# Attention two batches at a time, single heads on 64 partitions, 32-blocks solved by outer products, the order set by a list scheduler

## The chip, the core and the metric

The kernel runs on one core of a Trainium2 chip. A core has TensorE (PE, with weight loads shown as PEld), VectorE (DVE), ScalarE (ACT), GpSimd (POOL) and SyncE (SP), which here does nothing but issue DMAs. The metric is the time of one execution in microseconds (us) on the device. Time before: median 1033.7 us over three runs (1032.56 to 1038.22).

## The reference

A recurrence over 768 tokens, for 4 batches and 8 heads of 40 channels, and then a product over all 3072 tokens of 320 channels:

```python
for t in range(S):                                   # S = 768, state is 40x40 per batch and head
    y[:, :, t] = np.einsum('bhd,bhde->bhe', rt, state)
    Sa = np.einsum('bhde,bhe->bhd', state, at)
    state_decay = state * wt[:, :, None, :] - np.einsum('bhd,bhe->bhde', Sa, bt)
    state = state_decay + np.einsum('bhd,bhe->bhde', vt, kt)
x = y.transpose(0, 2, 1, 3).reshape(3072, 320)
out = ((x @ w_a) * (x @ w_b)) @ w_out                # d_ff = 1536; the weights are float64
```

## The kernel before

The recurrence runs in 12 chunks of 64 tokens. For a chunk, *prep* forms the running products of the decays (scans `Pc`, `Qc` on DVE), multiplies them into a, b and k (`A`, `BK`), transposes b and k (`bkn`) and makes the scores of b and k against a. The scores of a head are a 64x64 triangular matrix; `I + it` has to be inverted. *lanes* inverts its two 32x32 diagonal blocks, *merge* makes the block beside them from two products, and *main* computes, in turn: `RH` (state and v met by a), `UV` (the inverse times that), `G` (masked products of r), `yn` (the output), the new state `ST`, and its transpose `SD`. *xform* and *expand* turn y into x, split in a high and a low float32r part (`xk`, 120 rows of three heads).

Before, each of the four batches is prepared and run by itself. Three heads share 120 partitions, and a product that must keep heads apart uses an operand that is laid out block-diagonally (`Abd`, the state `ST`, the decays `pcm`; POOL makes them). `lanes` has the 128 blocks of a chunk on lanes: 64 blocks, each on two lanes which take every second row. Its 31 steps are a multiplication (L504) and a subtraction (L507) on DVE. Its data goes out through DRAM and back (`nb_d` to `N`, `Y` to `ts_d` to `TT`).

The product after it runs in *units*: one tile of 128 of the d_ff channels for the 256 tokens of a chunk. A unit is 16 matmuls into `ab`, copies and one product on ACT and DVE (`asb`, `g`, `gh`), a subtraction on POOL (`gl`) and 6 matmuls into `po`. There are 12 tiles and 12 chunks: 144 units. The first four tiles (`F1 = 4`) run beside the attention; the sums are put into DRAM (`po_d`), as is x (`xk_d`). In the last stage x and sums are loaded again, and the other eight tiles run in groups of two, over all chunks. The float64 weights are decoded on the chip to a high and a low part, in 72 pieces of 192 or 160 columns (six operations on DVE, two on ACT, two on POOL); `fill_rows` copies some rows within SBUF (`wt<-wt`).

The order is written out by times: a table `DEF` gives each step of prep, lanes, merge, main and units an emission time within a chunk of 16 units of time, the steps are sorted by it (`events`), and the engines' instructions are emitted in that order. Lane steps wait in a list (`fill`) and go behind other DVE instructions one at a time. All DMAs are issued by SP, in program order; each waits for its inputs and for room at its target, and holds back what stands behind it.

Of the kernel before, what the change touches and what calls it, by code (L numbers as in the profile page):

```python
# [30 lines left out]
CW = NG * (C + 1)      # width of the decay part of a packed input tile  # L31
PW = CW + 1 + NG * 3 * C
F1 = 4         # d_ff tiles that run beside the attention
FG = 2         # d_ff tiles of a group afterwards

LIMIT = 2.0 ** 8       # sum of the squares of the factors, over 2^60, that the chunked form may meet

# emission times of the parts of a step, 16 to a step, 4 to a batch
DEF = {
# [8 lines left out]
}  # L48


class InOrder:
    """An engine whose instructions keep the order in which they are given; after() comes
    behind each."""

    def __init__(self, tc, eng):
        self.tc, self.eng, self.after = tc, eng, None

    def __getattr__(self, name):
        fn = getattr(self.eng, name)

        def call(*args, **kwargs):
            r = fn(*args, **kwargs)  # L62
            self.tc.keep_in_program_order(r)
            if self.after:
                self.after()
            return r
        return call


def token_by_token(tc, p, ps_at, pin, rv, done):  # L70
    """The recurrence as it stands, a token at a time; done(n, x) gets x^T of a chunk."""
    nc = tc.nc
    # 1 where row and column belong to the same head
# [8 lines left out]
    # identity for the rows of each head  # L82
# [30 lines left out]
    with tc.For_i(0, pin.shape[0], 1) as n:  # L113
        I = p.tile([PK, B, PW], F32, name="sI")
        nc.sync.dma_start(out=I, in_=pin[bass.ds(n, 1)].rearrange("n b p w -> p (n b) w"))
        # in the order of the packed input: v, r and, in the order of the other groups, b and k of the second
        V, R, BK = (p.tile([PK, B, x, C], F32, name=nm) for nm, x in (("sV", NG), ("sR", NG), ("sBK", 2)))
        for g in range(NG):
            for t, x in ((V, 4 if g == 1 else 0), (R, 3 if g == 1 else 4)):
                nc.sync.dma_start(  # L120
                    out=t[:, :, g], in_=rv[bass.ds(n, 1), :, :, (1, 0, 2)[g], x].rearrange("n b p t -> p (n b) t"))
        abk = I[:, :, CW + 1:].rearrange("p b (g x t) -> p b g x t", g=NG, x=3)
        for i in range(2):
            nc.vector.tensor_copy(out=BK[:, :, i], in_=abk[:, :, 1, 2 - i])
        nc.vector.tensor_copy(out=abk[:, :, 1, 1:], in_=BK)
        x = p.tile([PK, NG, B, C], F32, name="sx")
        w = I[:, :, 0:CW].rearrange("p b (g t) -> p b g t", t=C + 1)
        for t in range(C):
            a, b, k = (abk[:, :, :, i, t] for i in range(3))
            rs, vs = columns(R[:, :, :, t], "r"), columns(V[:, :, :, t], "v")  # L130
# [8 lines left out]
            nc.vector.tensor_mul(out=state, in0=state, in1=rows(w[:, :, :, t + 1]))  # L139
# [10 lines left out]
def wkv_moe(ctx, tc, pin, rv, vn, wa, wb, wo, out):  # L150
# [4 lines left out]
    WIDE = wo.dtype == I64  # L155

    const = ctx.enter_context(tc.tile_pool(name="const", bufs=1))
    dram = ctx.enter_context(tc.tile_pool(name="dram", bufs=1, space=DRAM))
    psab = ctx.enter_context(tc.tile_pool(name="psab", bufs=2, space=PSUM))
    pso = ctx.enter_context(tc.tile_pool(name="pso", bufs=2, space=PSUM))  # L160
    psa = ctx.enter_context(tc.tile_pool(name="psa", bufs=4, space=PSUM))

    def ps_at(name):
        return psa.tile([P, 512], F32, tag="at", name=name)
# [23 lines left out]
    # 1 where the row belongs to head j of its group  # L188
    m3 = const.tile([PK, NG], F32, name="m3")
    nc.gpsimd.memset(m3, 1.0)  # L190
    nc.gpsimd.affine_select(
        out=m3, in_=m3, pattern=[[-D, NG]], compare_op=ALU.is_ge, fill=0.0,
        base=0, channel_multiplier=1)
    nc.gpsimd.affine_select(
        out=m3, in_=m3, pattern=[[D, NG]], compare_op=ALU.is_gt, fill=0.0,
        base=D, channel_multiplier=-1)
# [4 lines left out]
    yid = const.tile([P, HB // 2, HB], F32, name="yid")  # L201
    nc.gpsimd.memset(yid, 1.0)
    for p in range(2):
        sl = yid[p * 64:(p + 1) * 64]
        nc.gpsimd.affine_select(
            out=sl, in_=sl, pattern=[[2, HB // 2], [-1, HB]], compare_op=ALU.is_equal,
            fill=0.0, base=p, channel_multiplier=0)
    sizes = const.tile([PK, 2 * B * NS], F32, name="sizes")
    usual = const.tile([1, 1], I32, name="usual")
    ones = const.tile([PK, 1], F32, name="ones")  # L210
    nc.gpsimd.memset(ones, 1.0)
    # DRAM scratch
    xk_d = [dram.tile([PK, 6, B * C], F32, name=f"xk_d{n}") for n in range(NS)]
    po_d = [dram.tile([2, P, DM], F32, name=f"po_d{n}") for n in range(NS)]
    nb0_d = [dram.tile([B * H, HB, HB], F32, name=f"nb0_d{n}") for n in range(NS)]
    nb1_d = [dram.tile([B * H, HB, HB], F32, name=f"nb1_d{n}") for n in range(NS)]
    ts_d = [dram.tile([2, B * H, HB, HB], F32, name=f"ts_d{n}") for n in range(NS)]

    def decode(pool, raw, rows, ncol, dst_hi, dst_lo):
        """High and low parts of float64 words, or of float32 values."""  # L220
        def t(name, dt=I32):
            return pool.tile([P, 192], dt, tag=name, name=name, bufs=2)[:rows, 0:ncol]

        def shaped(x):
            return x.rearrange("p (k f) -> p k f", k=3) if len(dst_hi.shape) == 3 else x

        if not WIDE:
            yield
            nc.scalar.copy(out=dst_hi, in_=shaped(raw))
            nc.vector.tensor_sub(out=dst_lo, in0=shaped(raw), in1=dst_hi.bitcast(F32))  # L230
            yield
        low, high = raw[:, :, 0], raw[:, :, 1]
        ex, mt, rs = t("w_ex"), t("w_mt"), t("w_rs")
# [3 lines left out]
        ts(out=ex, in0=high, scalar1=0x7FF00000, scalar2=None, op0=ALU.bitwise_and)  # L237
        nc.scalar.activation(out=ex, in_=ex, func=AF.Relu, scale=8.0, bias=bias[:rows])
        ts(out=mt, in0=high, scalar1=3, scalar2=0x007FFFF8, op0=ALU.logical_shift_left, op1=ALU.bitwise_and)
# [37 lines left out]
    def weights(dest):  # L277
# [4 lines left out]
        for i, (f, j, h) in enumerate(pieces):  # L282
            yield
            if begun:
                next(begun)
# [707 lines left out]
```

## Time and profile before

| | before |
|---|---|
| median of three runs | 1033.7 us |
| profiled execution, span | 1042.0 us, mean granted TensorE clock 0.899 |
| PE, PEld | 915.3 us (88%), 832.5 us (80%) |
| DVE | 692.4 us (66%) |
| ACT, POOL | 411.0 us (39%), 426.1 us (41%) |
| DMA | 103.29 MB in 135747 packets, 84922 of them under 512 B |

Busy times are those of one execution taken by the profiler; the time of a run is what the device takes without it. A row such as `L507 DVE TENSOR_TENSOR Y<-Y,Yt 128x126 ... x372 | 138.3, 372 | 8.5` is one group of instructions: line, engine, operation, output from inputs, partitions by elements of one form, count, busy us, mean ns of one, and idle time of its engine just ahead of it. In a row for a queue (`SPq`) three numbers are the shortest, the median and the longest duration of an issue in ns, which is the time that SP takes to hand over the DMA and not the time of its transfer. In a table by stretches each row has a stretch from:to in us, its length, the busy time of each engine with its count, the TensorE clock that was granted, the mean busy share of the 16 DMA engines, and GB/s.

### The profile page before, as it was taken

The page shows a single profiled execution, that of the slowest core. Times are in us where ns is not written, and L with a number is a line of the kernel's source. Part 1 is how long each engine was busy: PE and PEld are TensorE (multiplying, and loading weights), DVE is VectorE, ACT ScalarE, POOL GpSimd, SP SyncE. Part 2 cuts the span into 40 slices and gives each one's busy share as a digit, 9 for nine tenths or more (in the row PEclk, how much of TensorE's full clock was granted, in tenths as well). Part 3 has the DMA queues.
Part 4 walks back from the last instruction along what each step waited for, and adds up shares of the span by engine and source line. Part 5 has one row for each costly group of instructions (what it writes and reads, how often), then busy time and mean ns, then how long its engine had stood idle before and what let it go on. Part 6 is the DMA issues. An engine that isn't in the chain of part 4 may idle for free.

```text
span 1042.0 us, 23609 instructions
## 1 busy us (share of the span) xinstructions
PE 915.3 (88%) x8942; PEld 832.5 (80%) x8942; DVE 692.4 (66%) x1890; ACT 411.0 (39%) x1317; POOL 426.1 (41%) x655
## 2 busy tenths in 40 slices
PE   4347798799999999999999999998939999999997
PEld 3236687688888888888888888877939999999996
DVE  7849889887869694859695937256227676757322
ACT  2122454444444444444544433345314343334221
POOL 5423647444435443434443402034215454445321
PEclk9999757889999988898989879797969999999998
DMA  3344544727364636363636242343873110110111
GB/s 72 73 103 111 119 123 106 171 58 167 99 151 113 146 100 140 82 139 115 134 104 140 84 96 85 73 133 97 202 185 88 32 43 24 39 31 25 39 57 62
DMA packets 135747, 103.29 MB, mean 99 GB/s; under 512 B 84922, under 2 KB 125690, under 8 KB 135626
## 3 DMA queue, kind: packets, MB, share of 16 engines
q1 hardware_dynamic: 135626, 101.71, 39.6%
q8 instruction: 73, 1.20, 0.5%
q14 instruction: 48, 0.39, 0.1%
HBM read 77.77 MB, written 21.94 MB: 96 GB/s over the span
## 4 chain that ended last, share of the span: by engine, by line
PE 46%; DVE 31%; DMA 9%; issue 7%; POOL 4%; ACT 2%; SPq 1%; POOLq 0%; DVEq 0%; ACTq 0%
PE ab L62 21%; PE po L62 9%; DVE Y L507 8%; DVE Yt L504 6%; PE pss L62 3%; PE psy L62 3%; DMA wraw<-in_wa_dram 2%; DVE w_ex L62 2%; DVE G L62 2%; DMA xk<-xk_d 2%; PE psr L62 2%; DVE w_rs L62 2%; DVE w_mt L62 2%; DVE TT L62 2%; SPq L62 1%
## 5 line engine op out<-in xcount | busy, mean ns | idle before, releaser
L62 PE MATMUL ab<-xk,wt 120*128 120x256 f32 x2304 | 324.2, 297 | 0.0
L62 PEld LDWEIGHTS ab<-xk,wt 120*128 120x128 f32 x2304 | 309.2, 204 | 1.2 <-DMA xk<-lo 0.3
L62 POOL TENSOR_TENSOR gl<-g,gh 128x256 fp32r<-128x256 f32 x144 | 109.6, 761 | 311.4 <-ACT gh L62 311.4
L62 DVE TENSOR_TENSOR g<-ab,asb 128x256 f32<-128x256 f32 x144 | 61.0, 424 | 158.7 <-ACT asb L62 157.0
L62 PE MATMUL po<-wo,gh 128*128 128x320 f32 x576 | 162.0, 330 | 2.8 <-ACT gh L62 2.8
L507 DVE TENSOR_TENSOR Y<-Y,Yt 128x126 f32<-128x126 f32 (+22 forms) x372 | 138.3, 372 | 8.5
L504 DVE TENSOR_TENSOR Yt<-Y,N 128x126 f32<-128x126 f32 (+22 forms) x372 | 122.7, 330 | 26.6 <-DMA N<-nb_d 19.5
L62 ACT COPY asb<-ab 128x256 f32<-128x256 f32 x144 | 53.3, 370 | 185.9 <-PE ab L62 185.9
L62 PEld LDWEIGHTS po<-wo,gh 128*128 128x128 f32 x576 | 108.6, 199 | 4.1 <-ACT gh L62 3.7
L62 ACT CAST gh<-g 128x256 fp32r<-128x256 f32 x144 | 58.5, 406 | 102.7 <-DVE g L62 98.8
L62 PE MATMUL po<-wo,gl 128*128 128x320 f32 x288 | 93.7, 325 | 2.3 <-POOL gl L62 2.3
L62 POOL TENSOR_TENSOR pe<-Pc,rp 120x192 f32<-120x192 f32 x44 | 29.4, 668 | 158.0 <-DVE rp L62 149.1
L62 PE MATMUL pssc<-Abd,BK 120*128 120x192 f32 (+1 forms) x288 | 67.5, 383 | 11.0 <-POOL Abd L62 11.0
L62 PEld LDWEIGHTS pssc<-Abd,BK 120*128 120x128 f32 x288 | 60.5, 242 | 15.4 <-POOL Abd L62 15.2
L62 DVE TENSOR_TENSOR tmp<-pss,ST 120x360 f32<-120x360 f32 x44 | 23.2, 527 | 72.3 <-PE pss L62 70.3
L62 PE MATMUL psn<-ident,BK 120*128 120x120 f32 x144 | 31.1, 336 | 38.6 <-DVE BK L62 35.2
L62 PEld LDWEIGHTS po<-wo,gl 128*128 128x128 f32 x288 | 57.7, 200 | 4.6 <-POOL gl L62 4.0
L62 PE MATMUL psy<-bkn,G 128*64 128x40 f32 x768 | 49.7, 245 | 12.2 <-DVE G L62 12.2
L62 ACT ACTIVATE w_ex<-w_ex,bias 120x192 int32<-120x192 int32 (+1 forms) x72 | 32.1, 447 | 70.8 <-DVE w_ex L62 69.7
L62 PEld LDWEIGHTS psy<-bkn,G 128*64 128x64 f32 x768 | 48.1, 161 | 14.7 <-DVE G L62 14.7
L62 POOL TENSOR_TENSOR Abd<-A,m 120x576 f32<-120x576 f32 x48 | 56.2, 1172 | 7.1 <-DVE A L62 3.2
L62 PE MATMUL psg<-rvt 120*128 120x192 f32 (+1 forms) x288 | 55.9, 334 | 0.8 <-DVE xT L62 0.8
(93 smaller groups left out, 1650.3 us busy)
## 6 DMA issues: line engine op xcount, KB each, us to landing
rvt<-in_rv_dram SPq DMA_DIRECT2D x48, 450.0 KB
I<-in_pin_dram SPq DMA_DIRECT2D x48, 361.9 KB
xk_d<-xk SPq DMA_DIRECT2D x11, 720.0 KB
xk<-xk_d SPq DMA_DIRECT2D x11, 720.0 KB
N<-nb_d SPq DMA_DIRECT2D x48, 128.0 KB
wraw<-in_wa_dram SPq DMA_DIRECT2D x24, 180.0 KB
wraw<-in_wb_dram SPq DMA_DIRECT2D x24, 180.0 KB
wraw<-in_wo_dram SPq DMA_DIRECT2D x24, 160.0 KB
```

The lines of the kernel that those rows point to most:

```text
L62: r = fn(*args, **kwargs)
L504: lambda: nc0.vector.tensor_mul(out=Wv, in0=Y[:, 0:ni, s:s + 1].to_broadcast([P, ni, w]), in1=N[:, s:s + 1, s + 1:].to_broadcast([P, ni, w])),
L507: lambda: nc0.vector.tensor_sub(out=Y[:, 0:ni, s + 1:], in0=Y[:, 0:ni, s + 1:], in1=Wv))
```

## The change

Two batches (a *pair*, `c`) go together. A head stands alone on one half of 64 of the 128 partitions (40 used), eight heads to a half. The three-head block diagonals are gone: scores, r, u, g and y are products of 64x64, 64x40 and so on, where neighbours use different halves of the array. Decays (`pe`, `A`) move from POOL to DVE. What prep makes of a pair (`A_k`, the masked scores `TK`, `pe`, `bkn`) is written to DRAM in eight DMAs (`un_d`, 1.12 MB) and read again as one tile `un` when main needs it.

`lanes` now serves a group of up to two chunks at once (`GROUPS`): 128 blocks, one on each lane. A step subtracts an outer product from a whole block. DVE transposes of 32x32 bring the blocks to lanes and back, instead of DRAM. The inverted blocks reach `T` in four DMAs from SBUF to SBUF per chunk. Also from SBUF to SBUF: the state into `SV`, four DMAs per pair, and x into the 120-row `xk`, six for the high part (`XH`) and six for the low (`X`) per pair. Before, the only ones of this kind were two per chunk for x (`xk<-lo`) and two per tile of weights.

Weights are decoded in 36 pieces of 384 or 320 columns. Two more tiles (`FE = 2`) and four chunks of x are loaded as soon as prep's pools are closed. The units are as before, in halves of 8 matmuls each, so that other PE work may come between.

Instead of the table, each operation is handed to a list scheduler (`Plan`) with an assumed duration and latency, its inputs, and a rank. It takes the operation that can start first by these numbers (by rank among those within 0.05 us), and the order it finds is the program's. The core of the diff:

```diff
+NP = 2
+M = 8
+FE = 2
+GROUPS = ((0,), (1, 2), (3, 4), (5, 6), (7, 8), (9, 10), (11,))
+    def run(self, slack=0.05, switch=0.13):
...
+                s0 = min(s for s, _ in c)
+                s, o = min(((s, o) for s, o in c if s <= s0 + slack), key=lambda x: (x[1].v, x[1].seq))
...
+    def us(n, fixed=0.16, each=0.00106):
+        return fixed + each * n
@@ prep @@
-            Abd = pp.tile([PK, NG, 3, C], F32, tag="Abd", name="Abd")
-            nc.gpsimd.tensor_mul(
-                out=Abd, in0=A[:, :, None, :].to_broadcast([PK, NG, 3, C]),
-                in1=m3[:, None, :, None].to_broadcast([PK, NG, 3, C]))
+        pl.op("SP", 0.06, lambda: nc.sync.dma_start(out=W, in_=wd[n, c]), w=[kW], lat=2.6)
+        def ak(gq):
+            for j in range(2):
+                nc.sync.dma_start(out=AKd[half(gq), gq, j],
+                                  in_=A[half(j), gq * 4:gq * 4 + 4].rearrange("p i t -> p (i t)"))
+        def scores(ps=ps):
+            for i in range(4):
+                for kind in range(2):
+                    for gq in range(2):
+                        for j in range(2):
+                            m, r = mi(gq, i), hd(j)
+                            c0 = (kind * 4 + i) * C
+                            mul(AT[half(gq ^ kind), ps.first + j, c0:c0 + C], BK[r, m, gq ^ kind], A[r, m])
+        pl.op("PE", 1.86, scores, [kBK, kA], need=ps, mode="q", lat=0.1, w=[("sc", q), kAB, kTK])
@@ lanes @@
-                ni, w = s // 2 + 1, HB - 1 - s
+            ni, w = s + 1, HB - 1 - s
+            def step(s=s, ni=ni, w=w):
+                o = Wt[:, 0:ni * w].rearrange("p (i t) -> p i t", i=ni)
+                nc.vector.tensor_mul(
+                    out=o, in0=Yt[:, 0:ni, s:s + 1].to_broadcast([P, ni, w]),
+                    in1=Nt[:, s:s + 1, s + 1:].to_broadcast([P, ni, w]))
+                y = Yt[:, 0:ni, s + 1:]
+                nc.vector.tensor_sub(out=y, in0=y, in1=o)
@@ merge @@
+                    if n == 0:
+                        nc.scalar.copy(out=T[r, :, HB * k:HB * k + HB], in_=TC[r, x])
+                    else:
+                        nc.sync.dma_start(out=T[r, :, HB * k:HB * k + HB], in_=TC[r, x])
@@ main @@
+        pl.op("SP", 0.06, lambda: nc.sync.dma_start(out=UN, in_=un_d[q]), [("un", q, i) for i in range(5)], [kU], lat=4.0, v=v - 0.3)
+            def s0():
+                for gq in range(2):
+                    for j in range(2):
+                        nc.sync.dma_start(out=SV[hd(gq), gq, j], in_=ST[hd(j), :, gq, 0:D])
+            pl.op("SP", 0.24, s0, [kST], [kS], lat=2.6)
+        def packh():
+            for j in range(2):
+                s, d = hd(j), slice(j * D, (j + 1) * D)
+                nc.sync.dma_start(out=xf[d, 0:3, tk], in_=hf[s, 0:3])
+                nc.sync.dma_start(out=xf[d, 5, tk], in_=hf[s, 2])
+                nc.sync.dma_start(out=xf[2 * D:PK, j, tk], in_=hf[s, 3])
+        def packl():
+            for j in range(2):
+                s, d = hd(j), slice(j * D, (j + 1) * D)
+                nc.sync.dma_start(out=xf[d, 3:5, tk], in_=X[s, 0:2])
+                nc.sync.dma_start(out=xf[2 * D:PK, 3 + j, tk], in_=X[s, 3])
+                nc.sync.dma_start(out=xf[2 * D:PK, (2, 5)[j], tk], in_=X[s, 2])
+        pl.op("SP", 0.36, packh, [kXH], [("xkh", n % 2, c)], lat=2.6, v=v + 0.15)
+        pl.op("SP", 0.36, packl, [kX], [("xkl", n % 2, c)], lat=2.6, v=v + 0.15)
...
+        pl.op("SP", 0.06, lambda: nc.sync.dma_start(out=xk2[n].bitcast(F32), in_=xk_d[n]),
+              [("xkd", n), "early" if n < NE else "late"], [("xk2", n)], lat=3.5, v=v)
-        events.sort(key=lambda t: t[:2])
+    pl.run()
```

How it moves the DMAs that SP issues, before, around the end of a chunk: the loads of a batch's v (`UV`), r and v (`rvt`) and prep input (`I`), then the low halves of x and the packed x on its way to DRAM.

```order
L62 DMA UV_181<-in_vn_dram 64x200
L62 DMA UV_181<-in_vn_dram 64x120
L62 DMA rvt<-in_rv_dram 120x3x320
L62 DMA po_d_110<-ot 128x2x320
L62 DMA xk<-lo 40x256 x2
L62 DMA I<-in_pin_dram 120x772
```

And now, on SP, at the same place: the four copies to T, v for the first pair, the packed x of the chunk before, that pair's state, its r and v and its packed prep, and then the first packs of its x.

```order
L58 DMA T_190<-TC 32x16x32 x4
L58 DMA SV_191<-in_vn_dram 64x320 x2
L58 DMA xk_d_96<-xk_207 120x1536
L58 DMA SV_191<-ST_199 40x4x40 x4
L58 DMA rv_193<-in_rvf_dram 128x1024
L58 DMA un_187<-un_d_133 128x2184
L58 DMA xk_206<-XH_205 40x3x128
L58 DMA xk_206<-XH_205 40x128 x2
```

What moved: of the seven DMAs of the first piece two are copies within SBUF, of the sixteen of the second eleven. The same two rows of packs come again behind them for the other half, and six more from `X`, before the second pair's v and state. In all, SP issues 536 DMAs before and about 885 now.

On PE before, one batch's tail and the next one's scores stand around a unit's 16 matmuls (`pss` is the state, `psyt` the transpose of y, `psn` that of b and k, `pssc` the scores):

```order
L62 MATMUL pss<-UV_180,bkn 120x120 x3
L62 MATMUL ab_0_5620<-xk,wt_191 128x256 x16
L62 MATMUL psyt<-ident,yn 120x128
L62 MATMUL psyt<-ident,yn 120x64
L62 MATMUL psn<-ident,BK 128x120 x3
L62 MATMUL pssc<-Abd,BK 128x192 x2
L62 MATMUL pssc<-Abd,BK 128x128
```

Now, around the state of a pair (`AT` is the shared PSUM tile; `40x40` is the state):

```order
L58 MATMUL AT<-RH_196,T_189 64x40 x16
L58 MATMUL AT<-T_189,RH_196 40x64 x16
L58 MATMUL ab_65<-xk_206,wt_222 128x256 x8
L58 MATMUL ab_64<-xk_207,wt_216 128x256 x8
L58 MATMUL AT<-SV_191,un_187 40x40 x16
```

What moved: the unit's matmuls come in halves of eight between a pair's steps, and here the state's product stands behind the first half that takes the x of the newer chunk (`xk_207`, where `xk_206` is the older), so PE reaches it only when the packs of that x have landed.

More of the change, by code (lines that the diff above doesn't have):

```diff
@@ new lines, in decode @@
+        yield "ACT", act(ncol), lambda: nc.scalar.activation(
+            out=ex, in_=ex, func=AF.Relu, scale=8.0, bias=bias[:rows]), (), (K[0],), None
+        yield "DVE", us(ncol), lambda: ts(
+            out=mt, in0=high, scalar1=3, scalar2=0x007FFFF8, op0=ALU.logical_shift_left, op1=ALU.bitwise_and), (kr,), (K[1],), None
+        yield "DVE", us(ncol), lambda: ts(
+            out=rs, in0=low, scalar1=1, scalar2=None, op0=ALU.logical_shift_right), (kr,), (K[2],), None
+        yield "DVE", us(ncol), lambda: stt(
+            out=ex, in0=high, scalar=-2147483648, in1=ex, op0=ALU.bitwise_and, op1=ALU.bitwise_or), (kr,), (K[0],), None
@@ L275, in fill_rows, with tile_steps @@
         nc.sync.dma_start(out=wf[2 * D:, :, 2, :], in_=wf[0:D, :, 2, :])
[L277 to L287 removed]
+    npiece = 0
+    def tile_steps(f, w):
+        nonlocal npiece
+        wt, wot = w
+        for j in range(3):
@@ new lines, in wkv_moe, with unit, half, second @@
+    KT = ((0, 0), (3, 0), (0, 3), (1, 1), (4, 1), (1, 4), (2, 2), (5, 5))
+    mo = {x: [mp.tile([P, 256], F32R if x in ("gh", "gl") else F32, name=f"{x}{i}") for i in range(2)]
+          for x in ("asb", "g", "gh", "gl")}
+    nunit = 0
+    def unit(xk, kx, w, slot, first, last, done, v):
+        nonlocal nunit
+        i = nunit % 2
+        nunit += 1
+        ab, (asb, g, gh, gl) = AB2[i], (mo[x][i] for x in ("asb", "g", "gh", "gl"))
+        wt, wot = w
+        wk = [("wt", slot, 0), ("wt", slot, 1), ("wf", slot), ("wh", slot, 0), ("wh", slot, 1)]
+        def half(j):
+            for k, (kw, kxi) in enumerate(KT):
+                mul(ab[:, j, :], wt[:, j, kw, :], xk()[:, kxi, :], k == 0, k == 7)
+        for j in range(2):
+            pl.op("PE", 0.95, lambda j=j: half(j), [kx] + wk, [("ab", i)], v=v, mode="r", lat=0.1)
+        pl.op("ACT", 0.37, lambda: nc.scalar.copy(out=asb, in_=ab[:, 0, :]), [("ab", i)], [("asb", i)], v=v - 0.4)
+        pl.op("DVE", 0.42, lambda: nc.vector.tensor_mul(out=g, in0=ab[:, 1, :], in1=asb),
+              [("ab", i), ("asb", i)], [("g", i)], v=v - 0.4)
+        pl.op("ACT", 0.4, lambda: nc.scalar.copy(out=gh, in_=g), [("g", i)], [("gh", i)], v=v - 0.4)
+        pl.op("POOL", 0.76, lambda: nc.gpsimd.tensor_sub(out=gl, in0=g, in1=gh.bitcast(F32)),
+              [("g", i), ("gh", i)], [("gl", i)], v=v - 0.4)
+        def second():
@@ new lines, in unit, with ring @@
+        pl.op("PE", 0.9, second, [("gh", i), ("gl", i), ("wt", slot, 2), ("wh", slot, 2)], [("po", 0), ("po", 1)],
+              v=v - 0.2, mode="r", lat=0.1)
+        if last:
+            done(v)
+    actx, pctx, lctx, rctx = ExitStack(), ExitStack(), ExitStack(), ExitStack()
+    a1 = actx.enter_context(tc.tile_pool(name="a1", bufs=1))
+    pp = pctx.enter_context(tc.tile_pool(name="pp", bufs=1, side="right"))
+    def ring(pool, n, shape, name, dt=F32):
+        return [pool.tile(shape, dt, name=f"{name}{i}") for i in range(n)]
@@ new lines, in wkv_moe, with prepare @@
+    rank = {}
+    for gi, g in enumerate(groups_of_chunks):
+        for n in g:
+            rank[n] = g[0]
+    next_w = 0
+    tiles_ahead = {}
+    wv = [0.9 + 0.25 * f if f < F1 else NS - 3 + 0.3 * (f - F1) for f in range(NSL)]
+    for f in range(F1):
+        plan_tile(f, slots[f], f, wv[f])
+    prepared = set()
+    def prepare(n):
+        if n < NS and n not in prepared:
+            prepared.add(n)
+            for c in range(NP):
+                prep(n, c, rank[n] - 1.5 + 0.4 * (n - rank[n]) + 0.1 * c)
@@ new lines, in wkv_moe, with plan_lazy, steps @@
+    run_tail()
+    lazy = []
+    for f in range(F1, NSL):
+        lazy.append(f)
+    return_ops = []
+    def plan_lazy(f, v):
+        slot = slot_of(f)
+        made = {}
+        def steps():
+            if "it" not in made:
+                made["it"] = [s for s in tile_steps_at(f, slots[slot], base)]
+            return made["it"]
+        nonlocal npiece
+        base = npiece
+        npiece += 3
+        for k, (i, j, (eng, dur, fn, r, wr, lat)) in enumerate(tile_steps_at(f, slots[0], base)):
+            kw = {"lat": lat} if lat else {}
+            wr = [("wt", slot, j) if x[0] == "dst" and x[2] == 1 else x for x in wr]
+            if any(x[0] == "dst" for x in wr):
+                wr = list(wr) + [("wh", slot, j)]
+            r = list(r) + ["early"]
+            pl.op(eng, dur, lambda k=k, steps=steps: steps()[k][2][2](), r, wr, v=v, **kw)
+        pl.op("SP", 0.12, lambda: fill_rows(slots[slot][0]), [("wt", slot, j) for j in range(2)],
+              [("wf", slot)], v=v, lat=2.5)
@@ new lines, in wkv_moe, with xof, kx @@
+    for f in range(F1, NSL):
+        plan_lazy(f, wv[f])
+    groups = [list(range(f, min(f + FG, NF))) for f in range(F1, NF, FG)]
+    t = NS + 1.3
+    def xof(n):
+        return (lambda: XK_[n % 2]) if n == NS - 1 else (lambda: xk2[n])
+    def kx(n):
+        return ("xk", n) if n == NS - 1 else ("xk2", n)
+    step = 0.01
+    t = NS + 0.5
+    ahead = min(2, NS - 1)
+    last_done = False
+    planned = NSL
+    for kk, fs in enumerate(groups):
+        last = kk == len(groups) - 1
+        for n in range(NS):
+            if kk == 0 and n == ahead:
+                for f in range(F1):
+                    unit(xof(NS - 1), kx(NS - 1), slots[f], f, f == 0, f == F1 - 1, fin1(NS - 1), t)
+                    t += step
+                while planned < min(NF, NSL + F1):
+                    plan_lazy(planned, NS + 0.6 + 0.3 * (planned - NSL))
+                    planned += 1
+            for k, f in enumerate(fs):
+                unit(xof(n), kx(n), W(slot_of(f)), slot_of(f), k == 0, k == len(fs) - 1, fin2(n, last), t)
+                t += step
+        while planned < NF and slot_of(planned) in [slot_of(f) for f in fs]:
+            plan_lazy(planned, NS + 0.6 + 0.3 * (planned - NSL))
+            planned += 1
@@ L911, in all_tiles @@
-            w = weight_tiles(p, "s")
-            stream = weights(lambda f: w)
-            for f in range(NF):
-                for _ in range(8 if f == 0 else 7):
-                    next(stream)
-                moe.first(f"s{f}", xk, w, f == 0, f == NF - 1, store)
-                moe.second()
+            xf = xk.bitcast(F32)
+            nc.scalar.copy(out=xk[:, 0:2], in_=x[:, 0:2])
+            for k in (2, 5):
+                nc.scalar.copy(out=xk[:2 * D, k], in_=x[:2 * D, 2])
+            nc.vector.tensor_sub(out=xk[:, 3:5], in0=x[:, 0:2], in1=xf[:, 0:2])
@@ L919, in wkv_moe @@
+            for hf in range(2):
+                nc.scalar.copy(out=ot[:, hf, :], in_=PO[hf][:, 0:DM])
+            nc.sync.dma_start(out=out[bass.ds(n, 1)].rearrange("n f p d -> p (n f) d"), in_=ot)
         token_by_token(tc, p, ps_at, pin, rv, all_tiles)
```

1249 lines of the change are left out of this document (621 added, 628 removed), and 8 rows, old and new, of the table DEF.

## The prediction

> **What bounds the kernel now.** I read the clock and span of the core first, then the engines' table by stretches of time, then the chain of waits, then single rows of the queue. By stretches:
>
> ```profile
> core 0: us, PE busy (x) PEld busy (x) DVE busy (x) ACT busy (x) POOL busy (x), PEclk, DMA share, GB/s
> 100.00:200.00 100.00, 83.41 (x731) 70.65 (x730) 90.40 (x274) 44.79 (x150) 60.36 (x88) 0.71 0.54 128
> 300.00:350.00 50.00, 48.03 (x574) 42.47 (x573) 38.39 (x104) 23.75 (x82) 22.30 (x35) 0.93 0.57 134
> 695.00:800.00 105.00, 81.67 (x618) 77.83 (x618) 49.72 (x143) 35.50 (x102) 37.77 (x56) 0.84 0.65 159
> 850.00:1000.00 150.00, 148.81 (x1164) 147.71 (x1163) 88.52 (x223) 54.35 (x144) 64.42 (x93) 1.00 0.11 34
> ```
>
> In the stage with attention (the 300 to 350 row) PE is busy 48 of 50 us and DVE 38; at 100 to 200 it is DVE that is full, with the decoding of the first weights, and PE's granted clock is 0.71. In the last stage PE alone is full at clock 1.00. Between them, 695 to 800, PE is busy 82 of 105 us. The chain of waits gives the pace of a chunk and PE's timeline that of a unit:
>
> ```profile
> 327.83 1.25 DVE Yt L504
> ...
> 585.81 1.26 DVE Yt L504
> ```
>
> ```profile
> 899.80 2.04 PE L62 MATMUL ab<-xk,wt 120*128 120x256 f32 x16
> ...
> 902.57 2.04 PE L62 MATMUL ab<-xk,wt 120*128 120x256 f32 x16
> ...
> 905.33 2.04 PE L62 MATMUL ab<-xk,wt 120*128 120x256 f32 x16
> ```
>
> The same longest lane step returns after five chunks, so a chunk takes (585.81 - 327.83) / 5 = 51.6 us; a unit takes 2.77 us. Of the 144 units 44 run beside attention (11 chunks, four tiles) and 100 after it: 277 us. So of the profiled span of 1042.0 us, 765 go to attention and the hole behind it. SP, which issues every DMA, has no row among the busy engines, but its own rows show what an issue costs (minimum/median/maximum in ns):
>
> ```profile
> L62 SPq DMA_DIRECT2D xk<-lo x24: 747/772/837, 171.7 to 731.4; - x24
> L62 SPq DMA_DIRECT2D wt<-wt x24: 768/814/901, 121.9 to 958.8; - x24
> L62 SPq DMA_DIRECT2D UV<-in_vn_dram x96: 466/582/1589, 66.8 to 694.2; - x96
> L62 SPq DMA_DIRECT2D I<-in_pin_dram x48: 324/449/1517, 0.8 to 567.6; - x48
> L62 SPq DMA_DIRECT2D xk_d<-xk x11: 332/446/1577, 178.9 to 696.5; - x11
> L62 SPq DMA_DIRECT2D po_d<-ot x11: 386/400/416, 228.9 to 728.0; - x11
> L62 SPq DMA_DIRECT2D wraw<-in_wa_dram x24: 336/350/705, 75.9 to 921.8; - x24
> ```
>
> ```profile
> 300.45 0.47 SPq L62 DMA_DIRECT2D I<-in_pin_dram  x1
> 300.97 1.77 SPq L62 DMA_DIRECT2D N<-nb_d  x4
> 302.79 1.16 SPq L62 DMA_DIRECT2D UV<-in_vn_dram  x2
> ...
> 329.69 1.64 SPq L62 DMA_DIRECT2D xk<-lo  x2
> 331.42 0.45 SPq L62 DMA_DIRECT2D I<-in_pin_dram  x1
> ```
>
> Two things are to be seen. The two kinds that copy from one part of SBUF to another, the low halves of x and the weights' filled rows, cost 0.77 and 0.81 us of issue, though they carry 40 KB; a load of 362 KB from DRAM (I) costs 0.45. And issues stand one behind the other: two of xk<-lo take 1.64 us, and a next one starts 0.05 to 0.1 us after the one before. The program's 536 issues at these prices (0.35 to 0.9, on average 0.56) are some 300 of 1042 us, so none of this is on the path now.
>
> **The change: engines.** DVE's lane steps now cover two chunks at once:
>
> ```profile
> L507 DVE TENSOR_TENSOR Y<-Y,Yt 128x126 f32<-128x126 f32 (+22 forms) x372 | 138.3, 372 | 8.5
> L504 DVE TENSOR_TENSOR Yt<-Y,N 128x126 f32<-128x126 f32 (+22 forms) x372 | 122.7, 330 | 26.6 <-DMA N<-nb_d 19.5
> L62 DVE TENSOR_TENSOR g<-ab,asb 128x256 f32<-128x256 f32 x144 | 61.0, 424 | 158.7 <-ACT asb L62 157.0
> L62 DVE TENSOR_TENSOR_SCAN Pc<-I,one 120x195 f32<-120x195 f32 x48 | 28.2, 588 | 12.7 <-DMA I<-in_pin_dram 12.7
> L62 DVE TENSOR_TENSOR BK<-I,Qc 120x384 f32<-120x384 f32 x48 | 32.0, 667 | 0.0
> ```
>
> They cost 261 us, 21.8 a chunk. The new step works on (s+1) x (31-s) elements, 176 on average; by the row with 256 elements (424 ns) and the lane rows (330 to 372) I take 0.34 us: 62 x 0.34 x 7 groups / 12 chunks = 12.3 us a chunk, and 2 for the transposes. Preparation now takes four pieces of work per chunk down to two, each with scans of 521 elements (by the 588 ns for 195: 1.5 us each) and products of 1024 and 512 (by 667 ns for 384: 1.6 and 0.8): about 6 us a pair, 12 a chunk; masks, state and g add 8. DVE: 34 us a chunk, where 38 of 50 were busy.
>
> On PE the 64-row products stay, and the block-diagonal scores go. What one costs, from psu alone in the stretch above:
>
> ```profile
> 300.00:350.00 50.00, 3.08 (x64) 2.62 (x64) 2.29 (x8) 0.93 0.57 134
> L62 PE MATMUL psw<-W,TT 32*32 32x32 f32 x768 | 23.5, 207 | 13.8 <-DVE W L62 10.5 <-DVE xT L62 3.1
> ```
>
> 64 records are 32 products (two passes each): 96 ns a product, with the tail of each short run of eight in it. A pair of batches has 160 such products: 15.4 us is the upper bound; in runs of 16 and 32 where two halves of the array work side by side a tail weighs less, and with 60 ns it is 9.6. I take 10, with the transposes 10.7, so 21.4 a chunk; the 128 small products of a chunk cost 7.8 by psw's 31 ns a record, 2 if four run side by side, and I take 2.3. Four units are 11.1. PE: 35 us a chunk at full clock, 46 at the upper bounds, 38 at clock 0.93. So both engines get faster, and neither is what I expect to set the pace.
>
> **The change: SP.** Each pair adds, from SBUF to SBUF, 12 packs of x and 4 copies of state; with two pairs and 4 copies of T that is 36 a chunk, where two were. At 0.79 (between the two rows) they cost 28.4 us. Per pair there are 8 DMAs of 64 partitions (0.51, between UV and xk_d: 4.1) and 7 of 128 (0.45, by I: 3.2). Per chunk: 2 x (12.6 + 4.1 + 3.2) + 4 x 0.79 + xk_d and po_d 0.85 + 68 gaps of 0.05 = 47.2 us. SP's issues of a chunk hid under PE's 51.6 us till now; 47.2 doesn't hide under 38. Twelve chunks are 566 us, less 10 for what the first and last do without; the first four tiles add 12 x 0.35 + 8 x 0.81 = 11, and the second pair with the first x read back 7. Issue alone: 574 us.
>
> To this come stretches in which SP stands still. **Start:** ahead of the first state DVE has four preparations (24 us), the lane steps of the first group (21), the decoding of four tiles (12 pieces of six operations, by BK's 667 ns for 384 columns: 48) and small work, 100 us in all; the 100 to 200 row shows how decoding fills it. I put that state at 115 us. SP's issues ahead of it, counted in the new order at the prices above, are 71: 44. **Waits in the queue:** SP keeps its order, so a pack that waits for ACT's high half or POOL's low half holds up the next pair's state, r and v and the packed read behind it. I estimate 3 us for x ahead of that read, 2 for the packs ahead of xk_d and 3 because each DMA waits for the landing of the one eight before it: 8 us a chunk, 88 for eleven. Below nothing it can't be; above, a chunk's data set the bound. A chunk moves 10.2 MB (the packed prep of 1.12 MB a pair goes out and comes back, 4.5 MB a pair in all). The rows give 134 GB/s at a share of 0.57, 235 at full share: 43 us, and up to 20 more where transfers and issue don't overlap. **End:** behind the last state stand the last packs and T, about 70 us of which 50 are in the sum: 20. **Last stage:** 100 units of 2.77 and 8 for the last sums: 285.
>
> 574 + 44 + 88 + 20 + 285 = 1011 us of profile. The median of the runs stands to the profiled execution as 1033.7 to 1042.0, 0.992: **1003 us**. A chunk so takes 55 us, more than now, and what wins is the hole, in which weights and x are loaded earlier now. The time is even with the old where the waits reach (1042 - 923) / 11 = 10.8 us a chunk.
>
> The Trainium skill says otherwise of issue: "DMA: Bandwidth & Descriptors", section "Issuing engines are not separate DMA queues", holds that the sequencer's time to start a DMA is usually small beside the DMA itself. For I that fits; for the 40 KB copies the rows above have 0.77 us of issue, and 40 KB at 235 GB/s are 0.17. By that rule the SP term would vanish, and the time would be the first rival's.
>
> **Rivals.** (1) *Issue doesn't bind:* the small copies of 20 to 60 KB cost less than xk<-lo's, or waits and issue lie inside one another, and PE and DVE set the pace. 115 to the first state, 11 x 39, 20 for decoding that collides, 40 at the end, 285: 889 us, in a run 882. For it speaks that SP's idle time in the profile is large; against it that both rows of such copies have minima of 0.75 us, so nothing cheaper has been seen. (2) *Slower: the queue's waits, with the data behind them.* The packed prep leaves and returns through the same 16 engines as the little copies, whose issue waits for the landing of the one eight before; with 43 us of data against 47 of issue there is no slack, and a wait on either side is paid on both. At 16 us a chunk: 923 + 176 = 1099, in a run 1090; it decides from 10.8 on. For it: a share of 0.65 in the hole, where PE idles 23 of 105 us; against it: most of the new packets are long rows (2 to 9 KB), which move faster than the many under 512 B now. (3) *PE sets it after all:* with the upper bounds, 46 us, at clock 0.9 a pace of 51: 115 + 561 + 50 + 285 = 1011, in a run 1003, the same time as mine with another cause.
>
> **How the numbers follow.** The forecast has 0.41, its cause replaced by (3) 0.04, (1) 0.18, (2) 0.37. About 0.5% is what a measurement of this kernel can tell from no change. Forecast and (3), with waits between 4 and 13 us a chunk, span 960 to 1060: 0.33 faster, 0.04 same, 0.08 slower. (1) is all faster; (2) is 0.32 slower and 0.05 near the bound. Together 0.51, 0.09, 0.40. The range goes down to 905, as far as (1) with a pace of 41 us, and up to 1105, which holds waits up to 17 us; the likeliest's own is 960 to 1060.
>
> **What will show it.** SP's rows for the copies to xk and SV at 0.75 to 0.85 us each, with SP issuing more than 80% of the time between 150 and 650 us; a chunk's pace of 50 to 60 us; PE busy under 80% of that stretch with its clock falling under 0.9; the chain of waits there made of SP's issues and DMAs rather than of PE and DVE; no hole of 100 us before the last stage. Copies at 0.4 us or PE full at a pace under 42 us would prove me wrong towards (1); a DMA share over 0.9 with SP idle between its issues towards (2).

## The result and the profile after

The changed kernel takes 1174.7 us (median of four runs, 1171.2 to 1176.0), the kernel before beside it 1033.1: a ratio of 1.135, 95% interval 1.130 to 1.139. It is slower, on the side of rival (2) and beyond the range. The page of its profiled execution, by engines:

```profile
span 1173.4 us, 29555 instructions
PE 832.9 (71%) x12538; PEld 774.4 (66%) x12538; DVE 593.9 (51%) x1179; ACT 336.8 (29%) x795; POOL 230.3 (20%) x267
...
DMA packets 117389, 152.58 MB, mean 130 GB/s; under 512 B 48498, under 2 KB 85618, under 8 KB 114178
```

Every engine has less to do than before (PE 915, DVE 692, ACT 411, POOL 426 us), and the span is 131 us longer. By stretches (columns as before), the stage with attention and two pieces of the hole behind it, where x, sums and weights are loaded:

```profile
200.00:650.00 450.00, 316.54 (x5796) 285.35 (x5791) 216.08 (x398) 132.64 (x314) 45.86 (x48) 0.68 0.54 162
...
860.00:880.00 20.00, 16.55 (x129) 16.17 (x128) 8.90 (x17) 5.40 (x14) 11.22 (x13) 1.00 0.99 255
880.00:900.00 20.00, 1.20 (x10) 1.00 (x8) 0.00 (x0) 0.00 (x0) 0.60 (x1) 0.59 0.98 227
```

The kernel before, in the first of these stretches, and its row of the state:

```profile
200.00:650.00 450.00, 429.83 (x4971) 379.92 (x4971) 330.13 (x903) 205.72 (x705) 180.62 (x280) 0.89 0.48 116
L62 DVE TENSOR_TENSOR tmp<-pss,ST x44: 518/532/534, 95.6 to 676.6; 120x360 f32<-120x360 f32 x44
```

Beside attention PE was busy 96% of the time at a granted clock of 0.89, and is now busy 70% at 0.68; no engine is full, and the DMA engines stand at 0.54. SP's rows after the change:

```profile
L58 SPq DMA_DIRECT2D xk<-XH x144: 706/760/1412, 117.8 to 853.9; - x144
L58 SPq DMA_DIRECT2D xk<-X x144: 706/731/1172, 122.6 to 859.0; - x144
L58 SPq DMA_DIRECT2D SV<-ST x88: 767/786/2208, 109.7 to 782.0; - x88
L58 SPq DMA_DIRECT2D T<-TC x44: 590/629/2434, 156.0 to 758.4; - x44
L58 SPq DMA_DIRECT2D un<-un_d x24: 320/370/991, 31.9 to 783.4; - x24
```

The copies within SBUF cost what the prediction took from two rows of the old kernel. The copies of state (SV<-ST) also mark the chunks: the first is issued at 109.7 us, that of chunk 10 at 761.1, so a chunk takes 65.1 us; the last goes at 782.0, and 391 us follow. Before, DVE's step of the state (`tmp<-pss,ST`) ran from 95.6 to 676.6 us, 10.75 chunks at 54.0 us, and 365 followed. So of the 131 us some 14 come ahead of the first state, 91 between first and last, and 26 behind. The chain of waits shows how a chunk goes now (start, length, what):

```profile
662.30 1.22 DVE G L58
...
664.27 0.34 SPq L58
...
664.72 0.80 SPq L58
...
665.57 0.76 SPq L58
...
673.60 1.84 DMA xk<-X
...
675.57 0.69 DVE X L58
...
676.28 7.59 DMA un<-un_d
```

Twelve packs stand one behind the other from 664.72 to 673.56, then the landing of the last, then DVE's X of the other pair, then the read of the packed prep that had to wait for it.

### The profile page after: what moved, and what is told of

Same layout as the page of the kernel before. It is cut to its first block, busy times and chain, and to the rows that moved or that the text cites. A ratio compares the mean times of both kernels' runs of the same rounds, so it can differ in the third digit from the quotient of the medians.

```text
span 1173.4 us, 29555 instructions
## 1 busy us (share of the span) xinstructions
PE 832.9 (71%) x12538; PEld 774.4 (66%) x12538; DVE 593.9 (51%) x1179; ACT 336.8 (29%) x795; POOL 230.3 (20%) x267
## 3 DMA queue, kind: packets, MB, share of 16 engines
q1 hardware_dynamic: 117250, 150.62, 43.8%
## 5 line engine op out<-in xcount | busy, mean ns | idle before, releaser
L58 PE MATMUL AT<-SV,un 128*64 128x40 f32 (+1 forms) x1472 | 63.4, 259 | 76.5 <-ACT uT L58 18.7
L58 PEld LDWEIGHTS AT<-SV,un 128*64 128x64 f32 (+1 forms) x1472 | 57.6, 172 | 85.8 <-issue 27.3
L58 DVE TENSOR_TENSOR Yt<-Y,N 128x31 f32<-128x31 f32 (+15 forms) x217 | 85.9, 396 | 1.9
L58 DVE TENSOR_TENSOR Y<-Y,Yt 128x31 f32<-128x31 f32 (+15 forms) x217 | 80.3, 370 | 7.5
L58 POOL TENSOR_TENSOR X<-X,XH 128x512 fp32r<-128x512 f32 x24 | 33.3, 1389 | 236.8 <-ACT XH L58 170.1
L58 PE MATMUL AT<-ident,BK 128*128 128x128 f32 x192 | 40.5, 381 | 41.1 <-DVE TK L58 13.9
L58 PEld LDWEIGHTS AT<-ident,BK 128*128 128x128 f32 x192 | 33.4, 199 | 44.0 <-issue 23.1
L58 PE MATMUL AT<-RH,T 64*64 64x40 f32 x768 | 40.7, 281 | 24.0 <-DVE G L58 7.1
L58 PEld LDWEIGHTS AT<-RH,T 64*64 64x64 f32 x768 | 37.4, 194 | 29.1 <-DVE G L58 7.7
L58 DVE TENSOR_TENSOR BK<-BK,Q 128x1024 f32<-128x1024 f32 x24 | 29.2, 1215 | 45.1 <-DMA BK<-in_bk_dram 45.1
L58 POOL TENSOR_TENSOR w_mt<-w_mt,wt 120x384 f32<-120x384 f32 x24 | 26.6, 1110 | 128.9 <-ACT wt L58 128.9
```

## Experiments

For each run stand its time, and from its trace: the first copy of state, the pace (from there to that of chunk 10, by ten), SP's issue time within that stretch per chunk (the durations added up), and the time behind the last copy of state.

| kernel | us | ratio to before | first state | pace | issue a chunk | behind the last |
|---|---|---|---|---|---|---|
| changed kernel | 1174.7 | 1.130 to 1.139 | 109.7 | 65.1 | 46.0 | 391 |
| e1 packs by ACT | 1242.9 | 1.191 to 1.210 | 110.3 | 71.3 | 25.7 | 392 |
| e2 SP's prices | 1180.9 | 1.130 to 1.150 | 104.3 | 65.3 | 46.4 | 398 |
| e3 prep read twice | 1240.8 | 1.188 to 1.209 | 118.4 | 70.1 | 47.4 | 394 |
| e6 no low packs | 1091.1 | 1.045 to 1.062 | 113.4 | 56.9 | 37.0 | 387 |
| e7 two X | 1166.0 | 1.117 to 1.139 | 109.0 | 62.0 | 46.2 | 401 |
| e8 three prep tiles | 1200.2 | 1.151 to 1.173 | 111.5 | 66.9 | 45.7 | 392 |
| e9 both | 1193.2 | 1.144 to 1.167 | 107.2 | 66.7 | 46.2 | 409 |
| e10 both, prices | 1195.6 | 1.149 to 1.170 | 109.0 | 66.6 | 46.3 | 399 |
| e11 packs by POOL | 1129.0 | 1.089 to 1.106 | 112.2 | 60.4 | 27.0 | 397 |
| e12 packs by chunk | 1102.9 | 1.064 to 1.080 | 112.3 | 58.5 | 34.9 | 389 |
| e13 328 issues fewer | 1110.4 | 1.071 to 1.088 | 115.8 | 58.2 | 24.9 | 392 |
| e14 e13, prices | 1089.2 | 1.051 to 1.067 | 118.7 | 57.7 | 24.2 | 381 |
| e15 e14, five tiles | 1061.2 | 1.018 to 1.044 | 115.9 | 57.8 | 25.6 | 355 |
| e16 e14, PE prices | 1156.6 | 1.108 to 1.138 | 114.3 | 58.6 | 23.7 | 437 |
| e17 e14, no lanes | 1011.3 | 0.969 to 0.997 | 67.3 | 54.8 | 26.1 | 361 |
| e18 e15, late weights | 1076.5 | 1.047 to 1.062 | 118.6 | 57.2 | 24.9 | 375 |
| e19 e18, six tiles | 1058.9 | 1.031 to 1.047 | 115.5 | 60.8 | 25.0 | 315 |
| e20 e15, by rank | 1141.3 | 1.100 to 1.115 | 96.7 | 66.4 | 26.4 | 371 |

**SP's issues, the order, or the bytes.** Four runs:

```diff
# e1_act_packs (twelve packs of a pair)
-                nc.sync.dma_start(out=xf[d, 0:3, tk], in_=hf[s, 0:3])
+                nc.scalar.dma_start(out=xf[d, 0:3, tk], in_=hf[s, 0:3])
# e2_costs (and so for each kind)
-        pl.op("SP", 0.36, packh, ...
+        pl.op("SP", 4.7, packh, ...
# e3_un_twice: the operation that reads un_d[q] stands twice
# e6_no_low
-        pl.op("SP", 0.36, packl, [kX], [("xkl", n % 2, c)], lat=2.6, v=v + 0.15)
+        pl.op("-", 0.0, lambda: None, [kX], [("xkl", n % 2, c)], lat=0.0, v=v + 0.15)
```

> The twelve packs of x of each pair are issued by ACT instead of SP, 288 of 896 DMAs, and the scheduler places them in ACT's order at its old price of 0.36 us for six. Theory Q (SP's queue sets the pace of a chunk, by its issues and by the order in which it waits): SP loses 288 x 0.77 = 222 us of issue, ACT gains about as much and has room for it (27 us busy of 100), the pace falls from 65 us a chunk to 45 to 52, and the time from 1175 to 980 to 1050. Theory D (the transfers set it: 10 MB a chunk and the wait for the landing of the eighth DMA before): the bytes stay, so the time stays at 1150 or above.

> Only the scheduler's prices of SP's DMAs are changed, from 0.06 us to what the rows show (0.45 for one of 128 partitions, 0.6 for one of 64, 0.8 for a copy within SBUF); work and queues stay. Theory Q with order: the waits of SP (about 18 us a chunk) come from an order made for a queue that costs nothing; 594 us of issue stay, so the pace goes from 65 us to 52 to 60 and the time to 1060 to 1130. Theory D: the order changes little, 1150 to 1190.

> The packed prep of each pair is read twice, one read behind the other into the same tile: 24 issues and 27 MB more. Theory Q: 24 x 0.42 = 10 us of issue and some of the second read's landing in the path, 1180 to 1230. Theory D: 27 MB at 235 GB/s are 114 us, 1260 or above.

> The six packs of the low half of x of each pair are left out (the low rows of x stay zero, so the product misses its low part): 144 issues and 4 MB less, nothing put on another queue. Theory Q: 144 x 0.77 = 111 us of issue less, of which most comes back: 1060 to 1090. Theory D: 4 MB are 17 us: 1150 or above.

Taking 144 issues away gave 84 us, 0.58 us for an issue of 0.77, where theory D expected next to nothing: the queue is on the path (theory Q). Without those packs X also comes free sooner, so not all of the 84 us need be issue. The bytes weigh too: 27 MB more cost 66 us, between the two expectations, 5 us a chunk for two reads of 1.12 MB each (9.5 us at 235 GB/s). The new order with true prices changed nothing, as theory D had it; theory Q with a cure by order had 1060 to 1130. And e1 came out slower by 68 us, where theory Q had 125 or more to gain. Its ACT timeline tells why:

```profile
409.59 0.62 ACT L58 CAST XH<-X 128x512 fp32r<-128x512 f32 x1 [4.72 <-DVE X L58]
410.24 4.85 ACTq L58 DMA_DIRECT2D xk<-XH  x6
415.13 0.42 ACT L58 COPY SV<-AT 64x320 f32<-64x320 f32 x1 [4.92 <-DMA xk<-XH]
```

An issue takes 0.76 us on ACT (median) as on SP, and ACT's own stream stands still for it. The copy of u to SV, which the state waits for, stood 4.9 us behind six packs here; the trace has 11 such waits of SV, 62 us, 9 of `asb`, 50 us, and 7 of SD, 41 us. That SP lost 20 us of issue a chunk while the pace rose by 6 shows that it matters whose path the issues stand on, and not only their number on one queue.

**Buffers.** A third theory (R): a ring of serial steps through single buffers.

```diff
# e7_x2
-    X_ = ring(a1, 1, [P, 4, 2 * C], "X")
+    X_ = ring(a1, 2, [P, 4, 2 * C], "X")
# e8_nu3
-NU = 2
+NU = 3
```

> X and its high half XH, of which there is one buffer for both pairs, get one each; no DMA and no issue is taken away. Theory Q (SP's issues and their order set the pace): nothing to gain but order, 1150 to 1190. Theory R (a ring of serial steps through single buffers: DVE's X of one pair waits until the packs of the other have been issued, 9.3 us, and have landed, 1.9 us; behind X waits the read of the packed prep): one such wait of two a chunk goes, about 5 to 9 us in eleven chunks, 1080 to 1120.

> Three tiles for the packed prep instead of two (the room comes from W4, which now lies in rows of T3 that are no longer read), so its read no longer waits for the X of the pair before the last one. Theory Q: 1150 to 1190. Theory R: the read, 7 to 9 us from issue to landing once or twice a chunk, leaves the ring, 11 x 8 = 90 us: 1070 to 1110.

> Both of these buffers (room from one pe and one RH buffer instead of two). Theory Q: 1140 to 1190, since SP still has 594 us of issue. Theory R: 11 x 13 us less, 1020 to 1060, with SP then busy 90% of the stage with attention.

> The same with SP's measured prices in the scheduler's table. If both theories hold in part (buffers first, then the order), the order now pays: 980 to 1030. If order is worth nothing here either, within 1% of the one with both buffers alone.

Theory R had 1080 to 1120, 1070 to 1110 and 1020 to 1060 for the first three, and none came, so it falls as far as these plans show. Two X give 9 us, less than its runs lie apart (1153.6 to 1169.8, of which the trace is the fastest); a third tile for the packed prep makes it slower by 25, which theory Q didn't have either; both are slower by 19, and true prices leave them there (e10 within 1% of e9) at 66.6 us a chunk.

**Fewer issues on SP.** e11 gives the packs to POOL; e12 lays x of both pairs out so that 8 DMAs do for 24; e13 also leaves the copies to T to ACT, half of the state's to POOL, and writes A_k in two DMAs; e14 is e13 with SP's prices.

```diff
# e12_chunk_packs (after both pairs; XH has a fifth row, a second copy of head group 2)
+                nc.sync.dma_start(out=xf[d, 0:4], in_=hf[s, 0:4])
+                nc.sync.dma_start(out=xf[2 * D:PK, j], in_=hf[s, 4])
+                nc.sync.dma_start(out=xf[d, 4:6], in_=lf[s, 0:2])
+                nc.sync.dma_start(out=xf[2 * D:PK, 2 + j:5 + j:2], in_=lf[s, 2:4])
# e13_fewer
-                    if n == 0:
+                    if True:
                         nc.scalar.copy(out=T[r, :, HB * k:HB * k + HB], in_=TC[r, x])
+                    nc.gpsimd.tensor_copy(out=SV[hd(gq), gq, gq], in_=ST[hd(gq), :, gq, 0:D])
```

> The 288 packs of x are issued by POOL instead of SP; POOL is busy 10 us of 100 beside attention, so little stands behind them there. Theory Q by the price that the run without low packs gave (84 us for 144 issues, 0.58 us each): 288 x 0.58 = 167 us less, 1000 to 1040, if POOL's issue costs no more than 1.5 us each. Theory S (SP's issue is a part only; the pace is set by serial steps among engines whose TensorE clock has fallen): 1100 to 1170. What an issue on POOL costs, no row has shown so far.

> x of both pairs lies in one buffer, in an order in which the packs of a whole chunk are 8 DMAs with rows of 1 to 4 KB, instead of 24 with rows of 512 B: 192 issues fewer on SP, nothing left out, one more short copy on ACT and one on DVE and POOL per pair. Theory Q: 192 x 0.58 = 111 us less, 1050 to 1090. Theory S: 1130 to 1180, since the packs of the first pair now come later.

> In addition the copies to T by ACT (44 issues), half of the state's copies by POOL (44), and A_k in two DMAs a pair instead of four (48): 328 issues fewer than in the changed kernel, 568 of 896. Theory Q: 190 us less, 970 to 1010, under the kernel before. Theory S: 1080 to 1150.

> The same with SP's measured prices in the scheduler's table. Theory Q: the order begins to count when the queue has slack; 0 to 30 us below the one without prices. Theory S: within 1% of it.

e11 gives 46 us and lies in theory S's range: POOL, which now has the packs in its order, keeps PE waiting for `gl` 33 us of the 450 from 200 to 650 (2.9 in e14). In e12 the first 192 issues give 72 us, which ends 13 us above theory Q's range and 27 below theory S's; each pair's X has room of its own there, too, as in e7. The next 136 give nothing (e13, 7 us slower than e12, in theory S's range). SP's prices then take 21 us off, which theory Q had and theory S had not, but the pace hardly moves (58.2 and 57.7), and half of it lies behind the last state. e6, e12 and e14 have 37, 35 and 24 us of issue a chunk and the same pace, 57 to 58.5. Theory Q ends there: below some 37 us of issue something else sets the pace. In e14 the chain of waits has neither SP nor a transfer in it for long stretches:

```profile
443.90 5.10 PE AT L58 x126
...
449.47 0.42 ACT SV L58
...
449.91 0.59 ACT uT L58
450.55 0.83 PE AT L58 x32
...
453.43 0.50 DVE tmp L58
...
455.96 2.00 PE ab L58 x8
457.97 4.50 PE AT L58 x128
...
462.49 0.59 ACT AB L58
...
463.88 0.69 DVE TK L58
464.57 0.67 DVE X L58 x2
...
475.67 1.05 PE ab L58 x8
```

PE, ACT, PE, DVE, PE: short steps in turn. A half unit (`ab` x8) takes 2.00 us at 455.96, where a whole one of 16 took 2.04 in the last stage before, and 1.05 at 475.67. The stretch from 200 to 650 us in e14 and, behind it, in e15 and in e20 (below):

```profile
200.00:650.00 450.00, 343.25 (x6874) 311.65 (x6876) 259.16 (x491) 172.24 (x403) 75.11 (x105) 0.75 0.55 171
```

```profile
200.00:650.00 450.00, 347.25 (x6996) 314.46 (x6994) 284.04 (x538) 181.64 (x425) 89.40 (x120) 0.81 0.57 177
```

```profile
200.00:650.00 450.00, 298.08 (x5994) 269.44 (x5998) 241.70 (x443) 158.14 (x375) 81.71 (x105) 0.77 0.52 162
```

In e14 and e15 PE idles a quarter of the time, and what it does runs at 0.75 and 0.81 of the clock. e15 belongs to the three runs that look into this. Their theories: (a) PE idles between serial steps, (P) PE is full at the clock it gets, (b) the order is made for a PE faster than it is, (c) DVE's lane steps set the pace.

```diff
# e15_five_tiles (room from single pe and RH buffers, W4 in T3, tmp in RH)
-F1 = 4
+F1 = 5
# e16_pe_costs
+        o.dur = dur * (1.4 if eng == "PE" else 1)
# e17_no_lanes
-            pl.op("DVE", 2 * us(ni * w), step, ["N"], ["Y"])
+            pass
```

> The kernel with fewer issues and measured SP prices, with five first d_ff tiles beside attention instead of four (room from single buffers of pe and RH, from W4 in T3 and from tmp in RH's room): 11 units of 2.77 us move from the last stage into PE's idle time. Theory (a), PE idles between serial steps: the pace stays near 58 us a chunk or falls with a higher clock, and the time falls by 20 to 45 us from 1089. Theory P (PE is full at its clock): the pace grows by 3 to 4 us and the time stays within 10 us.

> The kernel with fewer issues and measured SP prices; in the scheduler's table all PE durations are multiplied by 1.4, since the granted clock beside attention is 0.7 to 0.75. Only the order changes. Theory (b): 20 to 50 us below 1089. Theory (a): within 1.5% of it.

> The same kernel without the 31 lane steps of each group (the triangular blocks are not solved, transposes and merge stay): 434 DVE instructions, 166 us in the changed kernel, 14 us a chunk, are gone. Theory (c): the pace falls by 8 to 14 us a chunk, 950 to 1010. Theory (a) without DVE: at most 40 us.

A fifth tile beside attention costs nothing there (57.7 and 57.8 us a chunk) and takes 26 us from behind: theory (a) holds, PE's idle time is free for work that is there. Without the lane steps (e17, which so leaves work out) the time falls by 78 us, to the edge of theory (c)'s range, but the pace by 3 us only; 51 of the 78 us come ahead of the first state, so in the steady stage DVE is not the bound. PE prices for a slow clock made it worse by 67 us, which neither theory had; 56 of them lie behind the last state. The last runs:

```diff
# e18_late_weights
-            r = list(r) + ["early"]
+            r = list(r) + ["early"] + ([("xk2", 7)] if f >= NSL and eng == "SP" else [])
# e19_six_late: F1 = 6, one BK buffer, one set of the decoding's temporaries
# e20_by_rank
-    pl.run()
+    pl.run(slack=0.12)
```

> The kernel with five first tiles; the words of the tiles behind the first seven are loaded only when the eighth chunk's x has been read back, so no decoding on DVE waits behind the x and the sums of the last stage. If the hole is DVE held by that decoding, the 12 us in which PE idles around 804 to 820 go and the time falls by 8 to 20 us from 1061. If the hole is the 9 MB themselves (DMA share 1.0 at 250 GB/s), it moves and the time stays within 5 us.

> The same with six first tiles (room from one buffer each for BK and for the decoding's temporaries instead of two). If PE's idle time takes them at no cost, 11 x 2.77 = 30 us less than with five, 1010 to 1030; if the single buffers hold up the preparation or PE is full, not below the one with five tiles.

> The kernel with five first tiles, where the scheduler goes by rank among all operations that could start within 0.12 us instead of 0.05 us. In the order the first group's lane steps then stand behind one decoding operation instead of 22. If these stood in their way, the first state comes at 80 to 100 us instead of 116, and the time falls by 15 to 35 us to 1025 to 1045, which could meet the kernel before. If the first state is held by something else, 1050 to 1070.

e18 met neither of its two cases: it is 15 us slower than e15, with 20 more behind the last state. What it meant to cure is seen in the changed kernel on DVE (the last row is e18's):

```profile
877.07 0.54 DVE L58 SCALAR_TENSOR_TENSOR w_rs<-w_rs,w_ex 120x384 f32<-120x384 int32 x1
901.98 0.36 DVE L58 TENSOR_SCALAR w_ex<-wraw 120x384 int32<-120x384 int32 x1 [24.37 <-DMA wraw<-in_wb_dram]
```

```profile
821.32 0.36 DVE L58 TENSOR_SCALAR w_ex<-wraw 120x384 int32<-120x384 int32 x1 [29.45 <-DMA wraw<-in_wa_dram]
```

DVE stood 24 us for words that lay behind x and sums at a DMA share of 0.98, and PE with it. Loading those words later only moved the wait, 29 us in e18, so how much of the hole the 9 MB alone make is open. A sixth tile takes 18 us from e18, not 30, since the pace rises to 60.8; whether PE or the single buffers are full there is open. e20 did what it was made for, the first state comes 19 us earlier, and lost 80 us: the same work in another order has a pace of 66.4 instead of 57.8. No version that does all of the work beats the kernel before; e15 and e19 come within 2 to 5%.

**What the order blurs.** The scheduler planned anew for every run, so the engines also take their work in another order than in the kernel it is compared with; no run kept the order fixed. In e20 order alone is worth 8.6 us a chunk, as much as e6 gained (8.2). What speaks for the queue all the same is the row of plans: with 46 us of issue a chunk on SP (changed, e2, e7 to e10) the pace is 62.0 to 66.9, with 24 to 37 and no pack on ACT (e6, e11 to e16, e18, e19) 56.9 to 60.8, and e20 alone lies outside. So the side is shown, and the exact price of an issue is not.

## Why the prediction was wrong

**What held.** The price of a copy within SBUF (0.79; measured 0.63 to 0.79 by kind) and SP's issue a chunk, without gaps: 43.8, measured 46.0 (of the whole, 574 us were counted with gaps, and the trace has 593.5 without, for 896 DMAs). The first state: 115, measured 110, though in part by luck: SP issued 47 us ahead of it where 71 were counted, and without the lane steps, counted at 21 us, it came 51 us earlier. The work of the engines: in e14 the 450 us hold 7.8 chunks, so a chunk has 343 x 0.75 / 7.8 = 33 us of PE work at full clock, where I took 35, and 33 of DVE, where I took 34. SP's issues on the chain, PE under 80% and a clock under 0.9 came as described; SP's share was 72% of the time from 150 to 650 us, not over 80.

**What failed.** The sum was 1011 us of profile and the trace has 1173, 162 more: -5 ahead of the first state, 131 between first and last, 36 behind. The factor 0.992 from profile to run, which took 8 us off, didn't hold either: the span is 1173.4 and the median 1174.7.

1. *The step "neither is what I expect to set the pace", with 38 us for PE and DVE.* It took the work of the busiest engine for the pace that is left when the queue gives way. With SP's issues halved and off the chain for long stretches the pace is 57.7 us, not 38, with the work that I had counted (33 us of work at 76% busy and clock 0.75 is 58 us; that is the same row read the other way). So even the forecast's own 55 us a chunk is under what was reached with SP out of the way, and rival (1), 882 us, isn't reached by taking issues away; that gave 1089. What the runs show in its place: attention is a row of short steps that pass between PE, ACT and DVE, PE idles at the handovers, and part of its work runs at half pace (eight matmuls of `ab` in 2.00 and in 1.05 us). Its granted clock fell from 0.89, at 96% busy, to 0.68 at 70%, with 0.75 at 76% in e14 and 0.81 at 77% in e15; the busy share alone doesn't set it, for e20 has 0.77 at 66%. A lower clock lengthens PE's steps on the chain. The Trainium skill, "TensorE: Matmul & The Clock Gate", Part 1, has the array's clock at half after idle windows and at full after busy ones; the two times of the same eight matmuls agree with it. No run here forced the clock alone, so how much of the 58 us is clock and how much handover is not shown.

2. *The term "Waits in the queue", 8 us a chunk.* It measured twice as much: of 65.1 us a chunk, issue is 46.0, gaps are 3.4 as counted, and the rest, 16, is SP standing still. Of the 131 us this is some 80; 39 more are a slip in the sum itself, which gives 55 us a chunk and yet leaves only 1011 - 115 - 355 = 541 us for the 10.5 chunks between the first and the last state; the remaining 12 are issue, 46.0 for 43.8, less what the last half chunk took under the pace. For the waits, I had summed three waits of SP as if the engines it waits for kept their own time; but SP waits for steps that are slow by point 1, and they wait for SP, as in the chain above, where X waits for the packs and the read of the packed prep for X. Against e14's 57.7 us the queue costs 7.4 us a chunk, about 75 us of the whole; e6, e12 and e14 gave 84, 72 and 85 back, each with an order of its own. Rival (2) had the side and the place right, and its 16 us a chunk too, though with the same slip and the same end its sum came to 1090 only. Its cause, data and issue without slack, is right only in part: the share was 0.54, not over 0.9, and doubling the read of the packed prep cost 5 us a chunk.

3. *The term behind the last state, 70 and 285, and "what wins is the hole".* It measured 391 instead of 355. Early loading covers four chunks of x and two tiles; seven x and eleven sums still come at once, and the decoding on DVE stands behind them. PE is busy 86 of the 140 us from 780 to 920, where in the hole before it was busy 82 of 105. In e15 this part fell to 355 only by one tile's worth of units. Against the kernel before, where it was 365, the hole was not won.

By the Trainium skill's rule on issue time, "DMA: Bandwidth & Descriptors", "Issuing engines are not separate DMA queues", the time would have been 882 us; the rows of the small copies disagree with it (0.73 to 0.79 us of issue for 20 to 60 KB). The same page of the Trainium skill, "Rules for kernel authors", says to coalesce small transfers, since under 64 KB overhead is most of the cost; e12 agrees, with 72 us for 192 DMAs fewer, made of copies of 20 to 60 KB.

## What to carry to other kernels

Here a copy of 20 to 160 KB within SBUF cost SP's queue 0.6 to 0.8 us, with little regard to what it carried, so count issues per queue as one counts matmuls, coalesce them, and put them on a stream that nothing urgent stands behind. When the bound of a stage is taken away, the next one need not be the work of the busiest engine: if steps pass from engine to engine, measure the chain, and look at the TensorE clock again, which fell here from 0.89 to 0.68. A list scheduler's plan is not the run: measured prices gave nothing twice (e2, e10) and 21 us once (e14), slower prices for PE lost 67 us (e16), and a small change of a rule lost 80; time several orders.

## What the runs showed of the hardware

An issue on POOL for the same packs is shorter than on SP, where the medians were 760 and 731 (e11; median in ns between shortest and longest):

```profile
L58 POOL DMA_DIRECT2D xk<-XH x144: 517/527/882, 121.7 to 807.7; - x144
L58 POOL DMA_DIRECT2D xk<-X x144: 517/527/703, 125.4 to 811.1; - x144
```

On ACT it was 0.76 us and held up ACT's own work. The price hardly depends on what is carried: 20 to 60 KB in rows of 512 B cost 0.73 to 0.76 us on SP, and e12's packs in rows of 1 to 4 KB had medians of 0.74 and 0.79; T's 64 KB in 512 pieces of 128 B cost 0.63.
